# Attention and greedy expert routing on one core: four of the 24 deferred turns of x move from the first routing search to the stretch ahead of it

## Chip, cores and metric

The kernel runs on one core of a Trainium2 chip, in one launch. The metric is device time in microseconds (us) of a whole execution; the median of the runs counts. The engines are called PE (TensorE, matmuls), DVE (VectorE), ACT (ScalarE), POOL (GpSimd) and SP (SyncE, here a queue that issues DMAs).

## What is computed

The reference is attention with a soft cap on the scores, and behind it a layer of eight experts to which tokens are given greedily.

```python
# attention: q, k, v are (8 batches, 12 heads, 448, 64)
scores = cap * tanh(q @ k.T / sqrt(64) / cap)
attn   = exp(scores - max); attn /= sum(attn) + 1e-9
x      = (attn @ v).transpose(0,2,1,3).reshape(3584, 768)

# experts: capacity 448 tokens each
logits = x @ w_gate                       # 3584 x 8
for idx in argsort(-logits.flatten()):    # best pair first
    tok, e = divmod(idx, 8)
    if not assigned[tok] and counts[e] < 448: assign tok to e
for e in range(8):
    out[mask_e] = relu(x[mask_e] @ w1[e]) @ w2[e]
```

## The kernel before

The attention part (`attention`, up to some 331 us of the profiled execution) goes through 24 groups of four heads, three groups to a batch of tokens. For each group PE makes scores (line 190, 195), ACT applies tanh and exp (196, 201), DVE adds the exponentials (207), and PE multiplies them with v (231). The result for a batch is `xT`, x with its 768 features on partitions. From `xT` and the sums PE makes the logits of the batch (252; for the very last group 167), which are turned token-major by four transposes with `ident` (267). DVE divides and adds them (273 to 289) and writes the routing keys of the batch (`propose_a`, 498 to 509; the last key is `r_VA`).

x itself must lie in DRAM (`xs`) token-major, so that an expert's tokens can be gathered. One **turn** does that for one pair of heads of one batch (`xt`, lines 26 to 57): four PE transposes into one PSUM bank (37), then a copy out of the bank. For the batches 0 to 3 this happens inside the attention loop. For the last four batches (`NDEF=4`) it is deferred: 24 turns, each with the four transposes into a `psL` bank, a copy by ACT to a buffer `raw` (49), a multiply by POOL with the reciprocals `rin` into `xn` (52), and after some of them a write `xs<-xn` from the SP queue (56). Only the last turn of all is done by ACT alone (43) with a write from ACT's own queue (44). Batches 4 and 5 had been spilled to DRAM (`xd`) and are read back as `xTr` (30), both at the first deferred turn.

The deferred turns fill the first routing search. A search finds the threshold of the best 448 tokens of an expert in three phases A, B and C of 5, 6 and 5 steps (`select`). Here a step is named by phase and number: A1 to A5, B1 to B6, C1 to C5. A step is a chain: DVE and ACT compare the turned keys with three thresholds and count (`cmpD`, `cmpA`, lines 560 to 566), PE adds the counts over partitions (572, "the count"), DVE picks the next threshold (576, `fl`). Ahead of A1 PE turns the keys `r_VA` (536) and DVE casts them (534). In phase B, and just ahead of it, four matmul pieces of attention that are left over (`avs`, line 236 into `psX`) are issued in single steps, one each behind the counts of A5, B2, B4 and B6. After C5 `finalise` makes the token list `idx` (722), POOL gathers the tokens (871), and the first expert's matmuls (894, 965) begin.

The order is written out by hand: within `tc.manual_schedule` each engine executes in the order of the code. The loop of `ffn_all` sets how many turns are issued behind the count of each step:

```python
N0=1; UN=[1,2,1,2,1,2,1,2,1,2,1,2,1,1,2,0]; AN=(4,6,8,10)
...
step()
units(2)
while len(res)<1:
    step()
    if rt.pos=='B':            # behind a count
        if not deferred: warm(2)
        if m in AN: ...        # a left-over piece of attention
        units(UN[m%len(UN)]); m+=1
    elif rt.pos=='A': posts()  # behind the compares: the copies of the turns issued before
```

So ACT's copies of a step's turns stand behind ACT's compare of the next step. There are two `psL` banks and four `raw` buffers.

Of the kernel before, what the change touches and what calls it, by code (L numbers as in the profile page):

```python
# [14 lines left out]
DL=1; DD=[4]  # L15
FA=2
EB=3
def attention(nc, tc, c1, xp, ep, nv, pM, q, k, v, cap, w_gate, xs, L1, ident, on_logits, on_turn, NDEF, xd, setup, mark):

    B,H,S,D=q.shape
# [1 line left out]
    N=B*NQ  # L24
    xT={}; rin={}; xn={}; spilled={}; todo=list(range(B-NDEF,B-2))
    def xt(b,p,late=None):
        if late and todo:
            for n in todo:
                xT[n]=late[1].tile([128,NP,S],F32,name="xTr",bufs=len(todo))
                nc.sync.dma_start(xT[n],spilled[n])  # L30
            todo.clear()
        if p==0:
            alt=late and (b in spilled and (b-B)%2 or b==B-1)
            xn[b]=(late[1] if alt else xp).tile([CP,NJ,H,D],F32,name="xn",bufs=1)
# [24 lines left out]
    with ExitStack() as ctx:  # L59
# [247 lines left out]
        for g in range(N):  # L307
# [53 lines left out]
            if g: av_out(g-1,0); av_out(g-1,1)  # L361
            if m==2 and late and b<B-1: logit(bb,0,3)
        g=N-1; b=B-1
        rnd(b,R[0],True,False); rnd(b,R[1],False,False); rnd(b,R[2],False,True)
        logit_in(b)
        vround(0); vround(1)
# [2 lines left out]
        lgs[b]=xp.tile([128,S],F32,name="lg",bufs=1); ps=misc.pop(B)  # L369
        nc.vector.tensor_copy(lgs[b],ps[:,:S])  # L370
        ps=pT.tile([128,512],F32,name="psA")
        av(g,0,3,ps,3,2)
        logit(b,2,3,part=part)
        for j in range(3): av(g,0,j,ps,3,2)
    avs=[lambda ps,j=j: av(N-1,1,j,ps,0,3) for j in range(4)]
    return [lambda pool,b=b,p=p: xt(b,p,pool) for b in [B-2]+list(range(B-3,B-NDEF-1,-1))+[B-1] for p in range(NP)],avs


YL=[]
# [6 lines left out]
class Routing:  # L386
# [160 lines left out]
    def select(s,wp,Vt,ab,mid=None,post=None):  # L547
# [6 lines left out]
        for i in range(steps):  # L554
# [16 lines left out]
            ps=s.psum()  # L571
# [10 lines left out]
            if i==steps-1:  # L582
                s.tA=t0
                if ab=="C": s.row(s.tA)
            s.pos='B'; yield s.hB; s.pos=''
    def search(s,wp,turned=()):
        nc=s.nc; v=nc.vector
        post=None
        if s.cur==0:
            ps=s.spare(); s.cps={}; o=128  # L590
            for n in "ABC":
                S=s.steps[n]; s.cps[n]=ps[:,o:o+3*S].rearrange("p (s k) -> p s k",k=3); o+=3*S
                nc.scalar.activation(s.cps[n][:,1:],s.C[n][:,1:],AF.Copy)
        if turned:
            for h in range(s.NC//16):
                if ("VA",h) not in turned: s.turn("VA",h)
# [158 lines left out]


W1B=4; W2B=6
def ffn_all(nc, tc, ctx, rt, xs, xz, wg, w1, w2, out, ident, E, wp, deferred, xctx, gen, avs):
    C=448; DM=768; DC=6; DF=1024; FC=8; HD=384
    TS=[(0,128),(128,128),(256,128),(384,64)]  # L760
    wa=ctx.enter_context(tc.tile_pool(name="wa",bufs=W1B))
# [33 lines left out]
    rt.early=early  # L795
    zero_ix=wp.tile([16,1],I32,name="zix",bufs=1); nc.vector.memset(zero_ix,0)
    first_rows=wp.tile([16,E],F32,name="frow",bufs=1)
    N0=1; UN=[1,2,1,2,1,2,1,2,1,2,1,2,1,1,2,0]; AN=(4,6,8,10)
    ctx.enter_context(tc.manual_schedule(engines={ET.PE,ET.Activation,ET.DVE,ET.Pool,ET.SP}))
    pa=pt.tile([128,512],F32,name="psX")  # L800
    m=0
# [1 line left out]
    def warm(n,t=None):  # L803
        if not t:
            if not wu[0]: wu[0]=pt.tile([128,512],F32,name="psX")
            t=wu[0]
        for _ in range(n): nc.tensor.matmul(t[:,:128],ident,ident,start=True,stop=True)
    rt.warm=warm; rt.spare=lambda: wu[0]; rt.since=lambda: now[0]-end[0]; rt.place=lambda: now[0]%320
    warm(0)
    step()  # L810
    units(2)
    while len(res)<1:
        step()
        if rt.pos=='B':
# [249 lines left out]
def full(nc,tc,q,k,v,cap,wg,w1,w2,out):  # L1064
    with ExitStack() as ctx:
        cp=ctx.enter_context(tc.tile_pool(name="cp",bufs=1))
        dr=ctx.enter_context(tc.tile_pool(name="dr",bufs=1,space=bass.MemoryType.DRAM))
        xs=dr.tile([3584,768],F32,name="xs")
        NDEF=4
        xd=dr.tile([2 if NDEF<4 else NDEF-2,128,6,448],F32,name="xd")  # L1070
        xz=[dr.tile([n,768],I16,name=f"xz{i}") for i,n in enumerate((512,384))]
        ident=cp.tile([128,128],F32,name="ident"); make_identity(nc,ident)
        L1=cp.tile([112,32,8],F32,name="L1")
        r=Routing(nc,cp,3584,8); r.ident=ident; r.tc=tc
        xctx=ExitStack()
        xp=xctx.enter_context(tc.tile_pool(name="xp",bufs=2,side="right"))
        ep=xctx.enter_context(tc.tile_pool(name="ep",bufs=2,side="right"))
        nv=xctx.enter_context(tc.tile_pool(name="nv",bufs=5,side="right"))
        pM=xctx.enter_context(tc.tile_pool(name="pM",bufs=2,space=PSUM,side="right"))
        r.psum=lambda: pM.tile([128,512],F32,name="psM")  # L1080
        turned=set()
        def on_logits(b):
            (r.propose if b<7 else r.propose_a)(L1,4*b,4*b+4)
        def on_turn(b):
            if b==3:
                r.turn("VA",b//4); turned.add(("VA",b//4))
        r.mark=[None]
        deferred,avs=attention(nc,tc,cp,xp,ep,nv,pM,q,k,v,cap,wg,xs,L1,ident,on_logits,on_turn,NDEF,xd,r.setup,r.mark)
        wp=ctx.enter_context(tc.tile_pool(name="wp",bufs=2))
        pp=ctx.enter_context(tc.tile_pool(name="pp",bufs=2,space=PSUM))  # L1090
        r.pp=pp; r.pm=pM; del r.psum
        px=xctx.enter_context(tc.tile_pool(name="px",bufs=2,space=PSUM,side="right"))
        xr=xctx.enter_context(tc.tile_pool(name="xr",bufs=4,side="right"))
        deferred=[lambda f=f: f((px,xr)) for f in deferred]
        ffn_all(nc,tc,ctx,r,xs,xz,wg,w1,w2,out,ident,8,wp,deferred,xctx,r.phases(wp,L1,turned),avs)


_INS=["q","k","v","cap","moe_w_gate","moe_w1","moe_w2"]
# [24 lines left out]
```

## Time and profile before

| | us |
|---|---|
| median of 3 runs | 881.8 (880.81 to 882.2) |
| profiled execution, its own time | 885.21 |
| its span, first to last instruction | 883.4 |
| busy: PE / DVE / ACT / POOL | 858.3 / 587.2 / 585.2 / 374.3 |

The busy times are shares of the whole span: PE looks busy at 97%, but the chain of work that ended last runs through DVE, ACT, POOL and DMAs from some 327 to 387 us, where the attention ends and the experts' matmuls have not begun.

### The profile page before, as it was taken

To read this page: it belongs to the slowest core of one execution; us is meant where nothing else is said; L and a number is where in the kernel's file an instruction comes from. 1 tells how busy PE (TensorE), PEld (TensorE's weight loads), DVE (VectorE), ACT (ScalarE), POOL (GpSimd) and SP (SyncE) were. 2 spreads that over 40 slices of the span, in tenths; PEclk is the share of its full clock that TensorE was granted. 3 is DMA by queue.
4 is the path that set the end of the run, shared out by engine and by line. 5 is a ranking of instruction groups with operands and counts; after the bars stand their busy time and mean duration, and the time that the engine had idled before them with its cause. 6 is when DMAs were issued, how large, how long until landed. Compare 5 with 4: busy or idle time off the path is not lost.

```text
span 883.4 us, 17514 instructions
## 1 busy us (share of the span) xinstructions
PE 858.3 (97%) x6180; PEld 624.6 (71%) x6180; DVE 587.2 (66%) x2027; ACT 585.2 (66%) x832; POOL 374.3 (42%) x535
## 2 busy tenths in 40 slices
PE   6999999999999998989999999999999999999997
PEld 3334444444333435878988989989989989999997
DVE  3878898989897878756786777777767753130210
ACT  6999898989899968355384673664655745435521
POOL 8010000000000009464475496594674767756841
PEclk9999999999999999899999999999999999999999
DMA  9979998596995017770942883955935927929701
GB/s 136 153 121 148 187 138 166 94 181 97 227 181 83 1 57 246 203 221 1 287 125 54 220 263 111 262 164 161 279 111 171 310 81 192 309 66 243 229 10 53
DMA packets 339496, 140.05 MB, mean 159 GB/s; under 512 B 261232, under 2 KB 329456, under 8 KB 338896
## 3 DMA queue, kind: packets, MB, share of 16 engines
q1 hardware_dynamic: 328736, 109.03, 56.3%
q0 software_dynamic: 4688, 22.02, 7.4%
q10 hardware_dynamic: 5984, 7.88, 2.5%
q8 instruction: 48, 0.79, 0.4%
q14 instruction: 40, 0.33, 0.1%
HBM read 97.61 MB, written 33.03 MB: 148 GB/s over the span
## 4 chain that ended last, share of the span: by engine, by line
PE 84%; ACT 4%; issue 4%; DVE 3%; DMA 2%; POOL 1%; POOLq 0%; ACTq 0%; DVEq 0%
PE psH L965 26%; PE psH L996 25%; PE psA L231 12%; PE psS L190 11%; PE psM L252 3%; ACT e L196 2%; PE psS L195 2%; ACT e L201 2%; DMA w1r<-in_moe_w_dram 1%; PE psM L37 1%; DMA q<-in_q_dram 1%; PE psL L37 1%; PE psM L267 1%; POOL xg L871 1%; DVE cmpD L564 0%
## 5 line engine op out<-in xcount | busy, mean ns | idle before, releaser
L996 PE MATMUL psH<-w2h,hh 128*128 128x384 f32 x896 | 234.9, 340 | 0.0
L196 ACT ACTIVATE e<-psS 128x896 f32<-128x896 f32 x168 | 147.5, 910 | 30.0 <-PE psS L190 15.8
L996 PE MATMUL psH<-w2l,hh 128*128 128x384 f32 x512 | 165.8, 339 | 0.0
L996 PEld LDWEIGHTS psH<-w2h,hh 128*128 128x128 f32 x896 | 161.8, 188 | 0.1
L201 ACT ACTIVATE e<-e,bias 128x1792 f32<-128x1792 f32 (+2 forms) x74 | 147.3, 1991 | 1.8
L965 PE MATMUL psH<-xgh,w1h 128*128 128x448 f32 (+1 forms) x384 | 143.3, 373 | 0.1
L965 PE MATMUL psH<-xgh,w1l 128*128 128x448 f32 (+1 forms) x384 | 141.7, 369 | 0.0
L965 PE MATMUL psH<-xgl,w1h 128*128 128x448 f32 (+1 forms) x384 | 137.1, 370 | 0.0
L190 PE MATMUL psS<-tq,tk 64*64 64x448 f32 x1152 | 129.5, 544 | 7.5 <-ACT e L196 5.3
L849 POOL TENSOR_TENSOR w1l<-w1r,w1h 128x768 fp32r<-128x768 f32 x62 | 114.2, 1842 | 44.8 <-ACT w1h L842 42.5
L231 PE MATMUL psA<-e,nv 64*64 64x448 f32 x1104 | 120.8, 539 | 0.0
L849 POOL TENSOR_TENSOR w2l<-w2r,w2h 128x768 fp32r<-128x768 f32 x64 | 117.9, 1842 | 3.0 <-ACT w2h L842 2.9
L514 POOL TENSOR_SCALAR r_Bt<-r_b 112x4 f16<-112x4 int32 x1 | 0.2, 199 | 264.1 <-DVE rin L289 264.1
L207 DVE TENSOR_TENSOR es<-es,e 64x896 f32<-64x896 f32 (+2 forms) x70 | 96.0, 1372 | 2.7 <-ACT e L201 1.5
L996 PEld LDWEIGHTS psH<-w2l,hh 128*128 128x128 f32 x512 | 95.8, 188 | 0.1
L190 PEld LDWEIGHTS psS<-tq,tk 64*64 64x64 f32 x1152 | 42.8, 132 | 73.5 <-issue 36.8
L973 DVE SCALAR_TENSOR_TENSOR hh<-psH,hh 128x64 fp32r<-128x64 f32 (+1 forms) x128 | 44.1, 386 | 74.2 <-ACT hh L971 73.3
L971 ACT ACTIVATE hh<-psH 128x448 fp32r<-128x448 f32 x64 | 34.7, 542 | 84.6 <-PE psH L965 79.5
L231 PEld LDWEIGHTS psA<-e,nv 64*64 64x64 f32 x1104 | 44.5, 133 | 59.2 <-issue 51.6
L965 PEld LDWEIGHTS psH<-xgh,w1h 128*128 128x128 f32 x384 | 72.9, 190 | 8.0 <-issue 2.6
L965 PEld LDWEIGHTS psH<-xgh,w1l 128*128 128x128 f32 x384 | 72.7, 189 | 5.3
L965 PEld LDWEIGHTS psH<-xgl,w1h 128*128 128x128 f32 x384 | 72.7, 190 | 5.2 <-DVE xgl L928 0.2
(389 smaller groups left out, 1270.4 us busy)
## 6 DMA issues: line engine op xcount, KB each, us to landing
w1r<-in_moe_w_dram SPq DMA_DIRECT2D x64, 384.0 KB, 5.2
w2r<-in_moe_w_dram SPq DMA_DIRECT2D x64, 384.0 KB, 6.9
k<-in_k_dram SPq DMA_DIRECT2D x92, 112.0 KB, 3.4
q<-in_q_dram SPq DMA_DIRECT2D x92, 112.0 KB, 3.8
nv<-in_v_dram SPq DMA_DIRECT2D x72, 128.0 KB, 3.7
xz<-pl ACTq DMA_DIRECT2D x18, 384.0 KB, 3.0
xs<-xn SPq DMA_DIRECT2D x4, 1344.0 KB, 7.2
xd<-xT SPq DMA_DIRECT2D x2, 1344.0 KB, 6.1
```

The source lines that it names most:

```text
L37: nc.tensor.transpose(ps[:CP,j*128:(j+1)*128],xT[b][:,p,j*CP:(j+1)*CP],ident)
L190: for c in range(2): nc.tensor.matmul(ps[c*64:c*64+64,h,:S],tks[g,0][hp,o,u*128+c*64:u*128+c*64+64],tks[g,1][hp,o,:],start=True,stop=True)
L196: nc.scalar.activation(ev(g,r),ps[:,:,:S],AF.Tanh,scale=sr[0])
L201: act=lambda: nc.scalar.activation(e,e,AF.Exp,scale=sr[1],bias=bias)
L207: t=es_t[g]; add=lambda o,a,b: nc.vector.tensor_tensor(o,a,b,op=ALU.add)
L231: nc.tensor.matmul(avp[g,o][h*64:h*64+64,:S],lhs,rhs[hp,h,:],start=(j==0 and x==0),stop=j==3)
L252: nc.tensor.matmul(ps[g*32:g*32+32,:S],lhs,rhs,start=first,stop=last)
L849: (eng or nc.gpsimd).tensor_tensor(view(l),r,view(h).bitcast(F32),op=ALU.subtract)
L965: nc.tensor.matmul(ps[:,o:C],a[:,c,:],b[:,c,o:],start=(m==0 and o==0),stop=(m==DC*3-1)); m+=1
L971: nc.scalar.activation(h[:,:C],ps[:,:C],AF.Relu)
L973: nc.vector.scalar_tensor_tensor(h[:,d:d+b-a],ps[:,a:b],0.0,h[:,a:b].bitcast(F32),op0=ALU.max,op1=ALU.subtract)
L996: nc.tensor.matmul(ps[:,:HD],h[:,f,a:a+128],spl[p,2,hf,f//2][w][:,f%2,:],start=(m==0),stop=(m==nm-1))
```

## The change

The turns of batch 6 for the first four head pairs leave the search. The first stands ahead of the last group's first matmul with v (and so ahead of the transposes of the last logits), the second and third behind those transposes, the fourth (`held`) behind the last matmul with v. They use the PSUM banks of the attention scores (`psS`, two turns to a tile of two banks) and free `nv` buffers instead of `psL` and `raw`. The copy of the fourth is issued in `ffn_all`. The three small copies of constants by ACT (`consts`) move to a `psM` bank and behind the last logits. The other 20 turns are spread over the search with one or two to a step, and the last one stands in C5's place where `warm(2)` stood. The spilled batches are read back one by one: batch 5 at the first turn that is left, batch 4 at batch 6's last.

```diff
     def xt(b,p,late=None):
-        if late and todo:
-            for n in todo:
-                xT[n]=late[1].tile([128,NP,S],F32,name="xTr",bufs=len(todo))
-                nc.sync.dma_start(xT[n],spilled[n])
-            todo.clear()
+        if late and todo and len(late)<3 and (len(todo)==NDEF-2 or b==B-2 and p==NP-1):
+            n=todo.pop()
+            xT[n]=late[1].tile([128,NP,S],F32,name="xTr",bufs=NDEF-2)
+            nc.sync.dma_start(xT[n],spilled[n])
...
+        rest=[(bb,p) for bb in [B-2]+list(range(B-3,B-NDEF-1,-1))+[B-1] for p in range(NP)]
+        two=[None,0]
+        class Banks:
+            def tile(s,*a,**kw):
+                if not two[1]: two[0]=pS.tile([128,2,512],F32,name="psS")
+                two[1]^=1
+                return two[0][:,1-two[1],:]
+        class Rows:
+            def tile(s,*a,**kw): return nv.tile([128,3,2*HG,D],F32,name="nv").rearrange("p j h d -> p (j h d)")[:CP,:512]
+        def one(): return xt(*rest.pop(0),(Banks(),Rows(),False))
...
         ps=pT.tile([128,512],F32,name="psA")
+        u=one(); u()
         av(g,0,3,ps,3,2)
         logit(b,2,3,part=part)
+        consts(pM)
+        for _ in range(2): u=one(); u()
         for j in range(3): av(g,0,j,ps,3,2)
+        held=one()
...
+    def consts(s,pool):
+        ps=pool.tile([128,512],F32,name="psM"); s.cps={}; o=0
+        for n in "ABC":
+            S=s.steps[n]; s.cps[n]=ps[:,o:o+3*S].rearrange("p (s k) -> p s k",k=3); o+=3*S
+            s.nc.scalar.activation(s.cps[n][:,1:],s.C[n][:,1:],AF.Copy)
...
-        if s.cur==0:
-            ps=s.spare(); s.cps={}; o=128
-            for n in "ABC":
-                S=s.steps[n]; s.cps[n]=ps[:,o:o+3*S].rearrange("p (s k) -> p s k",k=3); o+=3*S
-                nc.scalar.activation(s.cps[n][:,1:],s.C[n][:,1:],AF.Copy)
...
-    N0=1; UN=[1,2,1,2,1,2,1,2,1,2,1,2,1,1,2,0]; AN=(4,6,8,10)
+    N0=1; UN=[1,1,1,2,1,1,1,1,1,2,1,2,1,1,1,1]; AN=(4,6,8,10)
...
-    warm(0)
     step()
-    units(2)
+    units(1)
+    held()
```

How this moves instructions is shown at three places. The first is PE from the last logits' matmuls (`vgs`) to the turn of the keys `r_VA`, before:

```order
L167 MATMUL psM<-e_3368,vgs 32x448 x8
L236 MATMUL psA<-e_3368,nvh 64x448 x2
L267 MATMUL psM<-ident,lg 112x128 x4
L236 MATMUL psA<-e_3320,nv 64x448 x2
L236 MATMUL psA<-e_3346,nv 64x448 x2
L236 MATMUL psA<-e_3368,nv 64x448 x2
L536 LDWEIGHTS r_VA
L536 MATMUL psR<-r_id_352,r_VA 128x112
```

The same stretch of PE in the changed kernel (its lines 235, 266 and 549 are the old 236, 267 and 536; line 36 is the old 37):

```order
L36 MATMUL psS<-ident,xT 112x128 x4
L235 MATMUL psA<-e_3368,nvh 64x448 x2
L266 MATMUL psM<-ident,lg 112x128 x4
L36 MATMUL psS<-ident,xT 112x128 x8
L235 MATMUL psA<-e_3320,nv 64x448 x2
L235 MATMUL psA<-e_3346,nv 64x448 x2
L235 MATMUL psA<-e_3368,nv 64x448 x2
L36 MATMUL psS<-ident,xT 112x128 x4
L549 LDWEIGHTS r_VA
L549 MATMUL psR<-r_id_352,r_VA 128x112
```

One turn (four transposes) now stands ahead of the last logits' transposes, and three more between them and the turn of the keys. With the counters that an instruction waits for, the turn of the keys reads in the changed kernel:

```order
L36 MATMUL psS<-ident,xT 112x128 [waits Activation_49]
L36 MATMUL psS<-ident,xT 112x128 x3
L549 LDWEIGHTS r_VA [waits DVE_49]
L549 MATMUL psR<-r_id_352,r_VA 128x112 [waits Activation_49]
L36 MATMUL psL<-ident,xT 112x128 x4
```

The `psR` bank that it writes is one that the fourth turn's `psS` tile held, and the count of ACT that it waits for is that of the fourth turn's copy; the corresponding matmul of before waits for nothing but DVE's `r_VA`. The second place is ACT in the same stretch, from the last exponential to the first compare, before:

```order
L201 ACTIVATE e_3368<-e_3368,bias 128x896
L593 ACTIVATE psX<-r_CA 128x12
L593 ACTIVATE psX<-r_CB 128x15
L593 ACTIVATE psX<-r_CC 128x12
L237 ACTIVATE xT<-psA 128x448
L560 ACTIVATE cmpA,r_cd_323<-r_VAt,r_T0A 128x252
L49 ACTIVATE raw<-psL 112x512 x2
```

and in the changed kernel (48 is the old 49, 236 the old 237, 573 the old 560):

```order
L200 ACTIVATE e_3368<-e_3368,bias 128x896
L48 ACTIVATE nv<-psS 112x512
L603 ACTIVATE psM<-r_CA 128x12
L603 ACTIVATE psM<-r_CB 128x15
L603 ACTIVATE psM<-r_CC 128x12
L48 ACTIVATE nv<-psS 112x512 x2
L236 ACTIVATE xT<-psA 128x448
L48 ACTIVATE nv<-psS 112x512
L573 ACTIVATE cmpA,r_cd_323<-r_VAt,r_T0A 128x252
L48 ACTIVATE raw<-psL 112x512
```

The four copies to `nv` are new here, and the fourth stands behind the copy of the last attention result and ahead of the first compare. The third place is the SP queue at the read-back, as a piece of the difference:

```order
-L30 DMA xTr<-xd 128x2688 x2
-L56 DMA xs<-xn 112x4x512
-L56 DMA xs<-xn 112x4x256
+L30 DMA xTr<-xd 128x2688
+L55 DMA xs<-xn 112x4x512
+L30 DMA xTr<-xd 128x2688
+L55 DMA xs<-xn 112x4x256
```

The second read-back now stands behind the first write of x, which waits for POOL's multiply of the fourth turn.

## Rows read from the trace of the kernel before

**Rows 1.** The chain of work that ended last, in order of time, from the last logits to the first expert: start us, us, what.

```profile
330.54 0.19 DVE r_VA L507
...
362.59 0.19 DVE idx L722
...
363.90 0.98 POOL xg L871
...
373.28 3.48 DMA w1r<-in_moe_w_dram
...
387.41 3.15 PE psH L965 x9
```

**Rows 2.** The timeline of PE from 326.5 to 331.3 us: start us, us, engine, line, operation, out<-in, count, and in brackets the idle time before and what ended it.

```profile
326.67 0.97 PE L236 MATMUL psA<-e,nvh 64*64 64x448 f32 x4
327.57 0.65 PE L267 MATMUL psM<-ident,lg 128*112 128x128 f32 x4
328.14 2.48 PE L236 MATMUL psA<-e,nv 128*64 128x448 f32 x12
330.79 0.22 PE L536 MATMUL psR<-r_id,r_VA 112*128 112x112 f16 x1 [0.17 <-DVE r_VA L507]
```

**Rows 3.** The timeline of all engines, same columns: DVE's copy of the last logits, the issue of the two read-backs on SP's queue, ACT's copy of the last attention result, two turns in one go ahead of A1's count, and one turn later on with ACT's copy behind it.

```profile
326.80 0.62 DVE L370 COPY lg<-psM 128x448 f32<-128x448 f32 x1
...
326.84 0.82 SPq L30 DMA_DIRECT2D xTr<-xd  x2
...
330.67 0.54 ACT L237 ACTIVATE xT<-psA 128x448 f32<-128x448 f32 x1 [7.27 <-PE psA L236]
...
331.26 1.09 PE L37 MATMUL psL<-ident,xT 128*112 128x128 f32 x8 [0.25 <-ACT xT L237]
...
338.64 0.65 PE L37 MATMUL psL<-ident,xTr 128*112 128x128 f32 x4
...
339.38 0.60 ACT L49 ACTIVATE raw<-psL 112x512 f32<-112x512 f32 x1 [0.19 <-PE psL L37]
```

**Rows 4.** The same timeline: the threshold picks of A1, A2, A3, then of B2 to B4 and B6, then of C4 and C5. Their distance is the length of a step.

```profile
332.52 0.16 DVE L576 SCALAR_TENSOR_TENSOR fl<-psR,r_HA 128x4 f32<-128x4 f32 x1 [0.27 <-PE psR L572]
...
333.92 0.16 DVE L576 SCALAR_TENSOR_TENSOR fl<-psR,r_HA 128x4 f32<-128x4 f32 x1
...
335.23 0.16 DVE L576 SCALAR_TENSOR_TENSOR fl<-psR,r_HA 128x4 f32<-128x4 f32 x1
...
341.02 0.16 DVE L576 SCALAR_TENSOR_TENSOR fl<-psR,r_HB 128x4 f32<-128x4 f32 x1
...
342.54 0.16 DVE L576 SCALAR_TENSOR_TENSOR fl<-psR,r_HB 128x4 f32<-128x4 f32 x1 [0.35 <-PE psR L572]
...
343.94 0.16 DVE L576 SCALAR_TENSOR_TENSOR fl<-psR,r_HB 128x4 f32<-128x4 f32 x1 [0.23 <-PE psR L572]
...
346.82 0.16 DVE L576 SCALAR_TENSOR_TENSOR fl<-psR,r_HB 128x4 f32<-128x4 f32 x1 [0.23 <-PE psR L572]
...
353.35 0.16 DVE L576 SCALAR_TENSOR_TENSOR fl<-psR,r_HC 128x4 f32<-128x4 f32 x1
...
354.76 0.16 DVE L576 SCALAR_TENSOR_TENSOR fl<-psR,r_HC 128x4 f32<-128x4 f32 x1 [0.24 <-PE psR L572]
```

**Rows 5.** The timeline of PE from the count of B2 to that of B3: count, left-over piece of attention, one turn, count.

```profile
340.81 0.18 PE L572 MATMUL psR<-r_cd,r_bo 128*128 128x4 bf16 x1
340.92 0.97 PE L236 MATMUL psX<-e,nv 128*64 128x448 f32 x4
341.82 0.65 PE L37 MATMUL psL<-ident,xTr 128*112 128x128 f32 x4
342.30 0.17 PE L572 MATMUL psR<-r_cd,r_bo 128*128 128x4 bf16 x1
```

**Rows 6.** Groups of instructions by line from 331.2 to 356.3 us, the search: line, engine, operation, names, shapes, count | busy us, mean ns | idle us before, and what ended it.

```profile
L52 POOL TENSOR_TENSOR xn<-raw,rin 112x512 f32<-112x512 f32 x23 | 23.3, 1049 | 0.1
L49 ACT ACTIVATE raw<-psL 112x512 f32<-112x512 f32 x23 | 12.8, 587 | 1.1 <-PE psR L572 0.9 <-PE psL L37 0.2
```

**Rows 7.** DMA issues by line in single narrow windows (KB each, median us from issue to landing): the first read-back, the second, the first write of x from SP's queue, and the last one from ACT's.

```profile
xTr<-xd SPq DMA_DIRECT2D x1, 1344.0 KB, 5.6
...
xTr<-xd SPq DMA_DIRECT2D x1, 1344.0 KB, 8.5
...
xs<-xn SPq DMA_DIRECT2D x1, 896.0 KB, 5.2
...
xs<-xn ACTq DMA_DIRECT2D x1, 448.0 KB, 3.7
```

**Rows 8.** Busy time of each engine in three stretches, phase A, the later phase C, and `finalise`: stretch, its length, busy us of PE, PEld, DVE, ACT and POOL, PE's granted clock as a share of full speed, the DMA engines' share, GB/s.

```profile
331.20:338.00 6.80, 5.47 (x43) 4.01 (x45) 5.70 (x39) 6.42 (x19) 6.47 (x12) 1.00 0.59 247
347.00:353.70 6.70, 4.75 (x37) 3.11 (x34) 5.43 (x35) 5.84 (x18) 6.70 (x7) 1.00 0.78 239
353.70:360.50 6.80, 6.18 (x31) 5.80 (x30) 4.68 (x25) 3.58 (x12) 3.39 (x4) 0.50 0.80 237
```

**Rows 9.** The timeline at the end of the search: ACT's eight small copies of the last turn, and in `finalise` DVE's last operand for the index matmuls and PE's load for the first of them, which stands behind 16 warming matmuls.

```profile
354.73 1.74 ACT L43 ACTIVATE xn<-psL,rin 112x64 f32<-112x64 f32 x8
...
359.39 0.42 DVE L706 TENSOR_TENSOR oi<-oh,r_idc 112x512 f16<-112x512 f16 x1
...
360.58 0.40 PEld L710 LDWEIGHTS <-oi 112*128 112x128 f16 x4
```

More of the change, by code (lines that the diff above doesn't have):

```diff
@@ L17, with attention @@
 EB=3
-def attention(nc, tc, c1, xp, ep, nv, pM, q, k, v, cap, w_gate, xs, L1, ident, on_logits, on_turn, NDEF, xd, setup, mark):
+def attention(nc, tc, c1, xp, ep, nv, pM, q, k, v, cap, w_gate, xs, L1, ident, on_logits, on_turn, NDEF, xd, setup, mark, consts):
     B,H,S,D=q.shape
@@ L371, in attention @@
         ps=pT.tile([128,512],F32,name="psA")
+        u=one(); u()
         av(g,0,3,ps,3,2)
         logit(b,2,3,part=part)
+        consts(pM)
+        for _ in range(2): u=one(); u()
         for j in range(3): av(g,0,j,ps,3,2)
+        held=one()
     avs=[lambda ps,j=j: av(N-1,1,j,ps,0,3) for j in range(4)]
-    return [lambda pool,b=b,p=p: xt(b,p,pool) for b in [B-2]+list(range(B-3,B-NDEF-1,-1))+[B-1] for p in range(NP)],avs
+    return [lambda pool,b=b,p=p: xt(b,p,pool) for b,p in rest],avs,held
 YL=[]
@@ L757, with ffn_all @@
 W1B=4; W2B=6
-def ffn_all(nc, tc, ctx, rt, xs, xz, wg, w1, w2, out, ident, E, wp, deferred, xctx, gen, avs):
+def ffn_all(nc, tc, ctx, rt, xs, xz, wg, w1, w2, out, ident, E, wp, deferred, xctx, gen, avs, held):
     C=448; DM=768; DC=6; DF=1024; FC=8; HD=384
@@ L807, in warm @@
         for _ in range(n): nc.tensor.matmul(t[:,:128],ident,ident,start=True,stop=True)
-    rt.warm=warm; rt.spare=lambda: wu[0]; rt.since=lambda: now[0]-end[0]; rt.place=lambda: now[0]%320
-    warm(0)
+    rt.warm=warm; rt.since=lambda: now[0]-end[0]; rt.place=lambda: now[0]%320
     step()
-    units(2)
+    units(1)
+    held()
     while len(res)<1:
@@ L1087, in full @@
         r.mark=[None]
-        deferred,avs=attention(nc,tc,cp,xp,ep,nv,pM,q,k,v,cap,wg,xs,L1,ident,on_logits,on_turn,NDEF,xd,r.setup,r.mark)
+        deferred,avs,held=attention(nc,tc,cp,xp,ep,nv,pM,q,k,v,cap,wg,xs,L1,ident,on_logits,on_turn,NDEF,xd,r.setup,r.mark,r.consts)
         wp=ctx.enter_context(tc.tile_pool(name="wp",bufs=2))
@@ L1094, in full @@
         deferred=[lambda f=f: f((px,xr)) for f in deferred]
-        ffn_all(nc,tc,ctx,r,xs,xz,wg,w1,w2,out,ident,8,wp,deferred,xctx,r.phases(wp,L1,turned),avs)
+        ffn_all(nc,tc,ctx,r,xs,xz,wg,w1,w2,out,ident,8,wp,deferred,xctx,r.phases(wp,L1,turned),avs,held)
 _INS=["q","k","v","cap","moe_w_gate","moe_w1","moe_w2"]
```

## Prediction, made without having seen the changed kernel run

> **What bounds the kernel now.** I read the chain of waits first, to see which part of the program the moved turns can touch. Between the attention and the first expert it does not run through PE's amount of work: it goes from the last logits' transposes over DVE to the keys `r_VA` (330.54), through the sixteen steps of the search to `idx` (362.59), then through the gather (363.90) and the expert's weights (373.28) to the first expert's matmuls (387.41) [rows 1]. The gather needs `idx`, so whatever moves `idx` moves all that follows by the same amount, and I price the change at `idx`.
>
> Next I read PE's timeline just ahead of the search, because three of the four turns go there, into what looks like a wait for the last logits. The reader is to see that this place is nearly full: the logits' transposes start at 327.57, the twelve matmuls with v at 328.14 and take 2.48, and the turn of the keys follows at 330.79, with a wait of only 0.17 for `r_VA` [rows 2]. The 2.65 us in which DVE makes the keys hold 2.48 us of matmuls. It is ACT that is idle there, 7.27 us before 330.67 [rows 3].
>
> Then the search. Two neighbouring picks of a threshold are 1.31 us apart where nothing disturbs (A2 to A3). The other distances are 1.40 (A1 to A2), 1.52 and 1.40 (B2 to B3 to B4), 2.88 for two steps (B4 to B6) and 1.41 (C4 to C5) [rows 4]. So most turns are hidden behind DVE's part of a step; what a thinner search can give back is bounded by these excesses over 1.31: 0.09 + 0.21 + 0.09 + 0.26 + 0.10 = 0.75, an estimate, as not every step has its row here.
>
> **The change, part by part.** *Turn 1* stands ahead of the last logits' transposes. These wait for DVE's copy `lg`, which ends at 326.80 + 0.62 = 327.42 [rows 3], and start at 327.57, when PE comes free: 0.15 us of room. A group of four transposes costs 328.14 - 327.57 = 0.57 from start to start [rows 2]. Nothing waits long enough to hide it, so the logits' transposes start at 328.14, and DVE's chain to `r_VA` ends at 330.73 + 0.57 = 331.30. That is the first term, and it is on the path by any reading but for the 0.15.
>
> *Turns 2 and 3* follow the transposes. Eight transposes in one go took 1.09 where four took 0.65 [rows 3], so 0.44 for each further turn, 0.88. The matmuls with v start at 328.14 + 0.57 + 0.88 = 329.59 and end at 332.07. *Turn 4* (`held`) follows at about 332.00 (a next group starts some 0.07 ahead of the modelled end: 326.67 + 0.97 against 327.57 [rows 2]) and ends 0.65 later, at 332.65.
>
> *The turn of the keys* now waits for ACT's copy of turn 4, as the order shows, since it writes a bank of that `psS` tile. ACT first copies the last attention result, 0.54 [rows 3], from about 332.12 to 332.66, then turn 4. A copy started 339.38 - (338.64 + 0.65) = 0.09 after its transposes and took 0.60 [rows 3]; I put it from 332.74 to 333.33. With 0.06 from that to PE, as from the end of `r_VA` (330.73) to 330.79 [rows 1, 2], the turn of the keys is at 333.39 instead of 330.79: **+2.60**. DVE's keys lie ready from 331.30, 2.1 us before. The stall has moved from DVE's chain to PE and ACT. Queued behind this matmul on PE are the first search turn and A1's count; behind the copy on ACT is A1's compare; DVE has nothing else to do.
>
> *The search.* Four turns fewer. A step that already has 1.31 gains nothing. A1 to A2 and C4 to C5 lose a double turn; I give each at most 0.1. A step with a left-over piece of attention is bound by PE: count, piece 340.92 to 341.82, turn 341.82 to 342.30, count [rows 5]; it keeps its piece and its turn, so it keeps its 1.52, and the step behind it too. B5 and C1 keep double turns. Sum: **-0.2**, against the other bound of -0.75.
>
> *POOL* multiplies four turns before it makes the keys of phases B and C. Its 23 multiplies of 1049 ns fill the search (23.3 us, idle 0.1), yet ACT's copies are held up by PE and not by POOL [rows 6]; with four done early it only gets ahead. I cost it at nothing. Those keys of B and C are read a whole phase later. *The constants'* copies lie in ACT's idle stretch; nothing.
>
> *The read-backs.* The first is issued as before, at 326.84 [rows 3], and lands 5.6 later [rows 7], ahead of its first use in A2. The second now stands on SP's queue behind the first write of x, which waits for POOL's multiply of turn 4, 333.4 to 334.4. The write lands 5.2 after its issue, and the second read-back of before, issued some 0.4 behind the first, landed 8.5 + 0.4 - 5.6 = 3.3 after it [rows 7]. That gives 334.4 + 5.2 + 3.3 = 342.9. It is first needed by the turn behind B2's count, before at 341.82 [rows 5], now at 341.82 + 2.6 - 0.1 = 344.3. Room of 1.4, so nothing; if it needed a full 8.5 behind the write, it would land at 348.1 and hold up PE, and with it the search, by 3.8. I take the first value, since the 8.5 of before holds the first read-back too, and none runs beside the second now.
>
> *The last write of x* starts behind ACT's eight copies, 1.74 us [rows 9], which now follow C5's turn and not C4's, one step (1.4) later. It lands 3.7 after its issue [rows 7], by my count 0.9 ahead of `idx`. Nothing, but this is the thinnest cover.
>
> **Sum.** +2.60 - 0.2 = +2.4. Against the profiled execution of 885.2 that is 887.6. It is 3.4 above the median of 881.8; I apply the same difference to the median: **884.2**.
>
> **A rule weighed.** In phase A PE runs hardly anything but transposes and counts, is busy for 5.47 of 6.80 us, and the granted clock is 1.00, its level of 2.4 GHz; behind the later phase C, busy for 4.75 of 6.70, it is 0.50, which is 1.2 GHz [rows 8]. Phase A has nine turns before and seven after, so PE's busy time there falls to about 5.47 - 2 x 0.44 = 4.6, close to that second row. That is the third rival below. The Trainium skill ("TensorE: Matmul & The Clock Gate", section "Part 4: PE-mode transpose") says that transposes do not count as PE activity in the way matmuls do; by that, taking some away would not change the clock, and the sum would stay 884.2. The row of phase A disagrees, as far as it goes: it holds its full clock on transposes. The same page's section "HAM oscillation — how this bites in real kernels" has the clock fall where PE is left waiting; by that the third rival would come true, and the 0.7 us that PE now waits ahead of the keys count for it.
>
> **The rivals.**
>
> *First, it is no slower: the turns fit in the waits.* If the three turns ran in PE's gaps and the fourth's copy were done before the keys are ready (331.30), only the 0.57 of turn 1 would stand against 0.2 to 0.75 from the search: +0.4 to -0.2, 881.6 to 882.2. It decides at the point where PE's added work between the logits' transposes and the keys, 0.88 + 0.57, with the copy behind it fits beside DVE's chain. Against it: 2.48 of the 2.65 us are taken [rows 2], and the order has a wait on ACT's copy. For it: modelled ends of PE, which may hide more room than the rows show, and ACT's 7.27 us of idle. Chance 0.21.
>
> *Second, the second read-back comes late* by part of the 0 to 3.8 us. At about half, 1.9: 886.1. For it: the wait behind a write that itself waits for POOL; against it the room of 1.4. Chance 0.07.
>
> *Third, the clock.* If it falls in phase A, a step with a left-over piece, 0.90 + 0.48 of PE work [rows 5], gets 1.38 longer. The low level lasted 6.8 us in [rows 8], enough for two such steps: +2.8, 887.0. For it the 4.6 of 6.8 above; against it that phase A is followed by the pieces themselves. Chance 0.06.
>
> *Fourth, faster.* `finalise` runs at half clock, and PE's load of `oi` starts at 360.58, 0.77 behind the end of `oi` at 359.81 [rows 9], held by warming matmuls. A turn in C5's place could keep the clock full and give back that 0.77 and more of the index matmuls behind it; with the first rival's sum that would be 880 or less. Alone, on the forecast's sum, it gives 883.4. Chance of the fast case 0.04.
>
> **How the numbers follow.** The forecast has 0.62. Its own range is 883.2 (the excess of 0.75 given back and another 0.4 of room on PE) to 885.4 (no saving, and some 1 us of the bounds above). 0.2%, 1.76 us, is about what a measurement of this kernel can tell from no change: below 880.0 is faster, above 883.6 slower. Of the forecast's 0.62 some 0.08 lie below 883.6. Faster: 0.05 with a remainder. Same: 0.21 + 0.08 = 0.29. Slower: 0.54 + 0.07 + 0.06 = 0.67, of which I take 0.66. The range reaches down into the first rival, to 881.4, and up to the second, 886.2; outside are the third, the fourth and half of the second's tail.
>
> **What would show it.** In the changed trace the last logits' transposes start some 0.57 later against the keys' chain, the turn of the keys at about 333.4 with ACT's `nv` copy as what ended its wait, the steps keep 1.31, 1.40 and 1.5, `idx` stands at about 365.0 and the first expert at 389.8. The second read-back lands before the turn behind B2 needs it, and the last write before `idx`. The prediction is wrong if the wait of the keys' turn is ended by DVE's `r_VA`, if the steps shrink below 1.31, or if the distance from `idx` to the first expert changes.

## The result, and the profile after

The changed kernel takes 886.5 us in the median (885.9 to 888.15, 6 runs), the kernel before on the same chip 881.35 (6 runs). The ratio is 1.0055, 95% interval 1.0045 to 1.0065: slower by 4.85 us by the ratio and by 5.15 by the two medians, where 2.4 was forecast. (881.35 x 1.0055 is 886.2, the figure that several texts below use for the changed kernel.) The sign and the mechanism at the keys are as forecast; the size is twice that. The 886.2 is the upper end of the prediction's range, and the median lies 0.3 above it.

The timeline of the changed kernel from the first moved turn to the search, PE and ACT's copy of the fourth turn (columns as in [rows 2]):

```profile
326.69 0.65 PE L36 MATMUL psS<-ident,xT 128*112 128x128 f32 x4
...
328.17 0.65 PE L266 MATMUL psM<-ident,lg 128*112 128x128 f32 x4
...
329.62 2.48 PE L235 MATMUL psA<-e,nv 128*64 128x448 f32 x12
...
332.02 0.65 PE L36 MATMUL psS<-ident,xT 128*112 128x128 f32 x4
...
332.71 0.60 ACT L48 ACTIVATE nv<-psS 112x512 f32<-112x512 f32 x1
...
333.36 0.21 PE L549 MATMUL psR<-r_id,r_VA 112*128 112x112 f16 x1 [0.69 <-ACT nv L48]
```

These answer to [rows 2]: the last logits' transposes at 328.17 (forecast 328.14), the matmuls with v at 329.62 (329.59), the fourth turn at 332.02 (332.00), its copy by ACT from 332.71 (332.74), the turn of the keys at 333.36 (333.39), its wait ended by that copy. The profile's chain of waits puts the start of the copy down to the landing of the first read-back (326.86 + 5.85 = 332.71). But the copy ahead of it on ACT ends only at 332.14 + 0.54 = 332.68, so the read-back can have held it by 0.03 us at most, and in a_both and a_mul_both below the chain has the transposes in that place.

DVE and POOL in the same stretch show what was not forecast:

```profile
329.96 2.09 POOL L51 TENSOR_TENSOR xn<-nv,rin 112x512 f32<-112x512 f32 x2 [0.80 <-ACT nv L48]
330.16 0.90 DVE L512 TENSOR_TENSOR r_P<-L,r_m 112x32 f16<-112x32 f32 x1
...
331.10 1.00 DVE L514 TENSOR_TENSOR r_P<-r_P,r_e8m 112x32 f16<-112x32 f16 x1
...
332.66 0.19 DVE L520 TENSOR_TENSOR r_VA<-r_P,r_At 112x32 f16<-112x32 f16 x1
```

Two operations of DVE take 0.90 and 1.00 us. POOL's two multiplies end at some 331.0 and at 332.05, and each of the two ends right behind one of them. `r_VA` starts at 332.66 and ends at 332.85, not at 331.30.

The picks of A1, A2, A4, A5, C4 and C5 and `idx`, as in [rows 4]:

```profile
335.01 0.16 DVE L589 SCALAR_TENSOR_TENSOR fl<-psR,r_HA 128x4 f32<-128x4 f32 x1 [0.27 <-PE psR L585]
...
336.31 0.16 DVE L589 SCALAR_TENSOR_TENSOR fl<-psR,r_HA 128x4 f32<-128x4 f32 x1
...
338.94 0.16 DVE L589 SCALAR_TENSOR_TENSOR fl<-psR,r_HA 128x4 f32<-128x4 f32 x1
...
341.02 0.16 DVE L589 SCALAR_TENSOR_TENSOR fl<-psR,r_HA 128x4 f32<-128x4 f32 x1 [0.91 <-PE psR L585]
...
356.53 0.16 DVE L589 SCALAR_TENSOR_TENSOR fl<-psR,r_HC 128x4 f32<-128x4 f32 x1
...
357.83 0.16 DVE L589 SCALAR_TENSOR_TENSOR fl<-psR,r_HC 128x4 f32<-128x4 f32 x1
...
366.20 0.19 DVE L735 TENSOR_REDUCE idx<-r_ixf 128x4 int32<-128x32 f32 x1
```

A1 to A2 fell from 1.40 to 1.30, as forecast. But A4 to A5 is 2.08 us, and C5 to `idx` is 8.37, against 362.59 - 354.76 = 7.83 in the first profile of before [rows 1, 4]. Busy time and clock ahead of and in the two places (columns as in [rows 8]):

```profile
330.50:337.30 6.80, 4.21 (x29) 2.15 (x25) 5.73 (x32) 4.02 (x11) 5.13 (x12) 1.00 0.48 160
351.00:357.80 6.80, 4.20 (x35) 2.90 (x33) 5.55 (x39) 6.01 (x18) 6.50 (x7) 1.00 0.82 252
357.80:364.60 6.80, 6.03 (x30) 5.57 (x31) 3.86 (x19) 2.67 (x10) 2.18 (x2) 0.50 0.55 163
```

PE is busy for 4.21 and 4.20 of 6.80 us in the first two stretches, and behind each the clock falls to 0.50 (1.2 GHz): from 337.35 to 340.76 and from 357.83 to 364.65. In the first fall the two turns of A4 show it, in the timeline and then in the chain of waits (start, us, what):

```profile
339.09 1.86 PE L36 MATMUL psL<-ident,xTr 128*112 128x128 f32 x8
```

```profile
339.30 1.65 PE psL L36 x8
```

In the timeline eight transposes took 1.09 us at full clock [rows 3] and take 1.86 here; DVE waits 0.91 us for the count behind them. In the second fall the chain runs through the 16 warming matmuls of `finalise`, which stand ahead of the index matmuls:

```profile
360.53 3.62 PE psX L820 x16
```

In the second profile of the kernel before, which comes next, it runs through DVE's `oi` in that place.

### The profile page after: what moved, and what is told of

The parts are those of the page before. It is cut to its first block, busy times and chain, and to the rows that moved or that the text cites. A ratio compares the mean times of both kernels' runs of the same rounds, so it can differ in the third digit from the quotient of the medians.

```text
span 884.1 us, 17509 instructions
## 1 busy us (share of the span) xinstructions
PE 857.3 (97%) x6176; PEld 624.2 (71%) x6176; DVE 589.0 (67%) x2027; ACT 586.6 (66%) x832; POOL 375.2 (42%) x535
## 4 chain that ended last, share of the span: by engine, by line
PE 80%; ACT 5%; DMA 5%; issue 4%; DVE 4%; POOL 1%; SPq 0%; ACTq 0%; POOLq 0%; DVEq 0%
PE psH L978 26%; PE psH L1009 22%; PE psA L230 11%; PE psS L189 10%; PE psM L251 3%; ACT e L195 2%; ACT e L200 2%; PE psS L194 2%; PE psM L36 1%; DMA xg<-xs,idx 1%; DMA q<-in_q_dram 1%; DVE es L206 1%; DMA xg<-xz 1%; DMA w1r<-in_moe_w_dram 1%; DVE cmpD L577 1%
## 5 line engine op out<-in xcount | busy, mean ns | idle before, releaser
L51 POOL TENSOR_TENSOR xn<-nv,rin 112x512 f32<-112x512 f32 x4 | 4.2, 1058 | 263.8 <-ACT psM L603 261.7
```

## The experiments

**b2: the kernel before, a second profile.** No edit.

> The kernel before, once more, for a second profile of it: its first one took 885.2 us where its median is 881.4. Expected: ratio 1.000, and a profile in which the stretch from the threshold search to idx is as in the first (idx at 362.6), while the time that is missing (some 3 us) shows behind idx, in the weight reads and the gather ahead of the first expert. If the search itself is shorter in the second profile, the comparison of the two first profiles is off by that much.

Median 881.76, ratio 1.0004 (0.9991 to 1.0017). The profiled execution took 882.5 us. Its clock stays full from 21 to 881 us, and the stretches of the first profile read (phase A, the later phase C, `finalise`):

```profile
331.60:338.40 6.80, 5.44 (x43) 4.00 (x45) 5.70 (x39) 6.42 (x19) 6.44 (x13) 1.00 0.59 246
348.30:355.10 6.80, 4.64 (x39) 3.34 (x37) 5.52 (x40) 6.01 (x19) 6.80 (x8) 1.00 0.77 239
355.10:361.90 6.80, 4.88 (x41) 4.26 (x41) 4.82 (x23) 2.51 (x10) 2.43 (x3) 1.00 0.88 251
```

The last picks and `idx` in it:

```profile
353.79 0.16 DVE L576 SCALAR_TENSOR_TENSOR fl<-psR,r_HC 128x4 f32<-128x4 f32 x1
...
355.09 0.16 DVE L576 SCALAR_TENSOR_TENSOR fl<-psR,r_HC 128x4 f32<-128x4 f32 x1
...
361.89 0.19 DVE L722 TENSOR_REDUCE idx<-r_ixf 128x4 int32<-128x32 f32 x1
```

Not all was as expected: C5 to `idx` is 6.80 us, not 7.83, and C4 to C5 1.30, not 1.41. Of the 2.7 us by which this profile's span is shorter (880.7 against 883.4), 0.7 lies up to `idx` and 2.0 behind it, where all of it was expected. So the first profile was of an execution in which the clock had fallen ahead of `finalise`, and of this kernel that is the exception: the mean clock over the 17 runs of it beside this one is 0.997 in the median, over the six of the changed kernel 0.992 (0.989 to 1.000 and 0.990 to 0.994).

Take this profile as the kernel before. From the turn of the keys (331.23 in this one, all of which runs 0.44 later than the first) the parts up to `idx` are:

| | forecast | changed against b2 |
|---|---|---|
| turn of the keys | +2.60 | 333.36 - (331.23 - 0.44) = +2.57 |
| keys to A4's pick | -0.1 | 5.58 - 5.75 = -0.17 |
| A4 to A5 | 0 | 2.08 - 1.30 = +0.78 |
| A5 to C5 | -0.1 | 16.81 - 16.81 = 0 |
| C5 to `idx` | 0 | 8.37 - 6.80 = +1.57 |
| sum | +2.4 | +4.75 |

Up to `idx`, then, half of the loss is the forecast's wait for the keys, and the other half is the two stretches in which the clock was low. That the sum is near the measured 4.85 is in part chance: the two profiled executions differ by only 3.4 us (885.9 and 882.5), because part of the 4.75 is given back behind `idx`. The chains of waits from the gather to the first expert, of b2 and then of the changed kernel:

```profile
365.98 6.13 DMA xg<-xs,idx
...
386.25 1.93 PE psH L965 x9
```

```profile
369.42 4.41 DMA xg<-xs,idx
...
389.30 1.93 PE psH L978 x9
```

From `idx` to the last of these rows, which is the row with which [rows 1] ends, it takes 24.82 us in the first profile, 24.36 in b2 and 23.10 in the changed kernel. Of the 4.75 some 3.5 arrive there (389.30 against 386.25 - 0.44).

For the whole time, what the clock costs is read from executions of one kernel. Among those of the kernel before that were taken beside the runs below, the seven with a mean clock of 0.993 took 882.8 us in the median, the 41 with 0.997 or 0.998 took 881.4. Of the changed kernel, the two with 0.990 took 887.2 and 888.2, the two with 0.994 took 885.9 and 886.2. By that the 0.005 between the two kernels' median clocks go with 1.6 to 2.0 us, an estimate; a part of the 4.85 stays unassigned.

**Three kernels with the second read-back where the change put it.** The first, a_three, sends the fourth turn back into the search:

```diff
-        held=one()
+        held=lambda: None
-    UN=[1,1,1,2,1,1,1,1,1,2,1,2,1,1,1,1]
+    UN=[1,1,2,2,1,1,1,1,1,2,1,2,1,1,1,1]
```

The second, a_mul, leaves the turns and moves POOL's multiplies of the early ones behind POOL's part of the keys; a_three_mul has both edits:

```diff
+            if late and len(late)==3: return lambda: mult(src,h0)
...
-        u=one(); u()
+        ms=[]; u=one(); ms.append(u())
...
-    held()
+    late.insert(0,held())
```

> The changed kernel with three turns ahead of the search and the fourth back in it (A3 gets two). The turn of the keys then no longer waits for the copy of a fourth turn. Theory 1 (the copy holds the keys by 0.45 us only, since DVE's keys are themselves late, 332.66, because two of DVE's operations took 0.90 and 1.00 us beside POOL's multiplies of the three turns): the turn of the keys at 332.9 instead of 333.4, and the time 0.4 to 0.5 us below the changed kernel's 886.2. Rival (DVE's two long operations are not tied to what POOL does there, or are not in the way): PE sets it, behind the matmuls with v, at 332.05, and the time falls by 1.3.

> The changed kernel with POOL's multiplies of the four early turns moved behind POOL's part of the keys; the turns and ACT's copies stay. Theory 1: DVE's two operations fall back from 0.90 and 1.00 to 0.19 each, r_VA is there at 331.2 instead of 332.66, but the turn of the keys still waits for ACT's copy of the fourth turn and stays at 333.36: the time changes by less than 0.2 us. Rival (what holds the keys is DVE and not the copy): the turn of the keys comes at 332.05 and the time falls by 1.3.

> Both of the last two edits: three turns ahead, and POOL's multiplies behind its part of the keys. Theory 1: neither ACT's copy nor DVE is in the way, and the turn of the keys comes where PE comes free of the matmuls with v, at 332.05: 1.3 us below the changed kernel, some 884.9, still 1.3 at the keys behind the kernel before. Rival (the two lateness terms add up and nothing else is there): 331.3 or earlier, 2.1 below the changed kernel.

All three came out slower than the changed kernel: 888.7 (ratio to before 1.0072), 889.3 (1.0091) and 891.1 (1.0108). At the keys they did what theory 1 says. In a_three, whose whole front runs 0.40 later than the changed kernel's, DVE's late keys are what ends the wait, at the 332.9 that was expected plus this 0.40 (the other two are repeated below without a second disturbance):

```profile
333.30 0.22 PE L549 MATMUL psR<-r_id,r_VA 112*128 112x112 f16 x1 [0.81 <-DVE r_VA L520]
```

But each made the first write of x later, and with it the second read-back behind it on SP's queue, issued at 336.53, 337.68 and 338.20 instead of 334.84. The turn behind B2's piece of attention then waits for it; this is a_three_mul, PE's timeline:

```profile
342.56 0.97 PE L238 MATMUL psX<-e,nv 128*64 128x448 f32 x4
347.99 1.07 PE L36 MATMUL psL<-ident,xTr 128*112 128x128 f32 x4 [4.46 <-DMA xTr<-xd]
```

In a_three the same wait is 1.99 us, in a_mul 1.76. The time from the read-back's issue to its landing in a_three:

```profile
xTr<-xd SPq DMA_DIRECT2D x1, 1344.0 KB, 9.6
```

In a_mul it is 10.0. In the changed kernel there is no such wait: the turn starts at 345.00, right behind the piece. Its landing is missing from this trace. In a_warm and a_warm2 below, which issue it where the changed kernel does, it took 9.8 and 10.0. At 9.6 to 10.0 it lands at 344.4 to 344.8 in the changed kernel, an estimate from those rows. The cover is 0.2 to 0.6 us, not the 1.4 of the prediction.

**The same with both read-backs at the front.** a_both is the changed kernel with this edit alone; a_mul_both and a_three_mul_both are two of the kernels above with it:

```diff
-        if late and todo and len(late)<3 and (len(todo)==NDEF-2 or b==B-2 and p==NP-1):
+        while late and todo and len(late)<3:
             n=todo.pop()
```

> The changed kernel with both read-backs issued at the front, ahead of the first write of x. In the changed kernel's trace the second read-back causes no wait (the turn behind B2 starts right behind the piece of attention, at 345.00), so theory 1 (it is free there): the time stays within 0.5 us of the changed kernel's 886.2. Rival (it is late in some executions; in three other kernels it landed 9.6 to 10.0 us after its issue, and by that would land at 344.4, only 0.6 ahead of its use): 0.5 to 1 us faster.

> The kernel a_mul (POOL's multiplies of the four early turns behind POOL's part of the keys) with both read-backs at the front. Its wait of 1.8 us for the second read-back behind B2 must go. Theory 1 (ACT's copy of the fourth turn holds the keys, whatever DVE does): the turn of the keys as in the changed kernel, 333.4, and the time as a_both's within 0.5 us. Rival: below a_both by 1 us or more.

> The kernel a_three_mul (three turns ahead, multiplies late) with both read-backs at the front. Its wait of 4.5 us behind B2 must go. Theory 1: the turn of the keys where PE comes free of the matmuls with v, 1.3 us ahead of the changed kernel's, and the time 1.3 below a_both's, if the clock behaves as there. If the clock stays full more often, up to 2 us below.

a_both: 886.3, ratio 1.0053 (1.0039 to 1.0066). The read-backs one by one cost nothing in the changed kernel, thin as the cover is.

a_mul_both: 885.97, ratio 1.0056 (1.0041 to 1.0071). Its DVE and its turn of the keys:

```profile
330.16 0.19 DVE L518 TENSOR_TENSOR r_P<-L,r_m 112x32 f16<-112x32 f32 x1
...
331.12 0.19 DVE L526 TENSOR_TENSOR r_VA<-r_P,r_At 112x32 f16<-112x32 f16 x1
...
333.35 0.21 PE L555 MATMUL psR<-r_id,r_VA 112*128 112x112 f16 x1 [0.69 <-ACT nv L48]
```

With POOL's multiplies out of the way DVE's operation takes 0.19 again and `r_VA` ends at 331.31, the forecast's 331.30. The turn of the keys does not move, and neither does the time: it is ACT's copy of the fourth turn that holds it.

a_three_mul_both: 883.94, ratio 1.0026 (1.0014 to 1.0039), 2.4 us below a_both. Without the fourth turn and with DVE free the keys come where PE is done with v:

```profile
332.11 0.22 PE L553 MATMUL psR<-r_id,r_VA 112*128 112x112 f16 x1
```

That is 1.35 ahead of a_both's 333.46, as expected (1.3). The other 1.0 is more than theory 1 had; 0.77 of it lies in the search up to `idx` (365.33 against 367.45 in a_both, 2.12 earlier), where the profiled a_both had its clock down for 6.8 us in phase A and a left-over piece of attention in that stretch, which took 1.76 us instead of the 0.97 of [rows 5]:

```profile
341.05 1.76 PE L235 MATMUL psX<-e,nv 128*64 128x448 f32 x4
```

That is the third rival's case as it was priced, in one execution. That the 1.0 comes from there is not shown: the two profiled executions differ by 0.6 us only (885.78 and 885.15).

**The clock.** a_warm adds idle matmuls ahead of the turn of eight steps, a_warm2 behind it, a_best puts the latter into a_three_mul_both (without the step A3, which has two turns there). The lines are those of a_warm2; a_warm has three and not four at B1 and B3:

```diff
-    AN=(4,6,8,10)
+    AN=(4,6,8,10); WM={0:4,1:4,2:4,5:4,7:4,12:4,13:4,14:4}
...
-            units(UN[m%len(UN)]); m+=1
+            units(UN[m%len(UN)])
+            warm(WM.get(m,0)); m+=1
```

> The changed kernel with three or four matmuls of ident with ident, whose results nothing reads, behind the counts of A1, A2, A3, B1, B3, C2, C3 and C4, where PE would wait. Theory 1 (a part of the loss is PE's clock, which in the changed kernel's trace stood at 1.2 GHz from 337.3 to 340.8 and from 357.8 to 364.7, and in the second profile of the kernel before nowhere in the search): the clock stays at 2.4 GHz, A4 to A5 falls from 2.08 us to 1.3, C5 to idx from 8.4 to 6.8, and the time falls by 2.3 us to some 883.9. Rival (the clock is a by-product and costs nothing): the time stays at 886.2, or grows by what the added matmuls delay the counts, 0.1 each.

> The kernel a_warm once more, with the four idle matmuls of a step behind its turn and not ahead of it: in a_warm they stood ahead of the turn, ACT's copy and its next compare came later by them, and the steps that held them took 1.43 to 1.47 us where they had taken 1.30. Theory 1 (the clock is the rest of the loss): full clock in the search as in a_warm, steps of 1.31 as in the changed kernel, C5 to idx in 6.8 us, and the time 2.3 us below 886.2, some 883.9. Rival (more PE work costs as much as the clock gives back, wherever it stands): 886 as a_warm.

> Every cause undone that the runs so far show, with three turns still ahead of the search: no fourth turn there, POOL's multiplies behind its part of the keys, both read-backs at the front (all as in a_three_mul_both, 883.9), and the idle matmuls of a_warm2. Theory 1: what is left is PE's work ahead of the keys, +1.3 us against the kernel before, less 0.2 in the search: some 882.5, a ratio of 1.001. Rival (something else in the change costs too): 883.9 as without the idle matmuls.

a_warm: 886.09, ratio 1.0046 (1.0032 to 1.0059). Mean clock 0.998, and full throughout the search and `finalise` in its profile; C5 to `idx` is 6.87 us and A4 to A5 1.34, as theory 1 has them. From the keys to `idx` it takes 31.41 us where the changed kernel takes 32.84. That is 1.43 and not 2.35, because the steps with idle matmuls take 1.43 to 1.47 where they had taken 1.30. Yet the median moved by 0.4 at most, and by the ratios by 0.8.

a_warm2: 885.55, ratio 1.0043 (1.0028 to 1.0058). The steps still take 1.38 to 1.42. The trace shows why:

```profile
335.24 1.06 PE L820 MATMUL psX<-ident 128*128 128x128 f32 x8
```

Four idle matmuls are eight instructions of PE and 1.06 us, so with the turn they fill the step. The turn behind B2 also waited 0.30 us for the second read-back. The clock fell only at 360.3, inside `finalise`, for 3.4 us.

a_best: 884.72, ratio 1.0036 (1.0020 to 1.0052); 882.5 was expected. It is no faster than a_three_mul_both without the idle matmuls (883.94), as the rival had it. The four of its twelve executions with a mean clock of 0.999 or more took 882.4 to 884.3, the others 884.4 to 887.6.

Where a_warm's gain at `idx` goes is seen in its chain of waits:

```profile
379.19 8.43 DMA w1r<-in_moe_w_dram
...
389.20 2.71 PE psH L979 x9
```

`idx` comes 0.95 us earlier than in the changed kernel, and the first expert's weights `w1r` are asked for 1.0 earlier (the changed kernel's row is 380.20, 7.53). But the read takes 8.43 us, so the matmuls behind it start only 0.1 earlier. Then the clock falls, and they take 2.71 us instead of 1.93. Such a last fall, for 3.4 us in the first expert, begins between 387.8 and 391.1 in the first profile of before, in a_warm, a_warm2 and a_best, and `idx` to the end of the span takes 520.6 to 521.2 us there; in the other ten profiles there is none, and the stretch takes 516.6 to 518.9. Why a kernel that kept its clock in the search should lose it there, no run tells apart. So a_warm shows what the clock costs up to `idx`, and not that holding it there is worth as much in the whole time: its five executions, with mean clocks of 0.998 to 1.000, took 885.05 to 887.66.

b_warm2 tried the idle matmuls in the kernel before.

```diff
+    AN=(4,6,8,10); WM={0:3,2:3,12:3,13:3}
...
+            warm(WM.get(m,0)); m+=1
```

> The kernel before with three idle matmuls behind the turn of A1, A3, C2 and C3. In most of its executions its mean clock is 0.997 or more, and in the one that was profiled first the clock fell ahead of finalise and C5 to idx took 7.8 us where the second profile has 6.8. Theory 1: it holds its clock already, so the median stays at 881.5 and at most the slower executions come nearer to it: ratio 0.999 to 1.000. Rival (the clock is lost in most executions): 1 us faster, 0.9988 or less.

887.21, ratio 1.0056 (1.0039 to 1.0073), and it says nothing on the clock: in the kernel before the constants of the search lie in the PSUM bank that the idle matmuls write, and DVE's compare reads them from there.

```profile
334.45 0.45 DVE L564 SCALAR_TENSOR_TENSOR cmpD<-r_VAt,th,psX 128x224 bf16<-128x224 f16 x1 [1.42 <-PE psX L807]
```

A1 to A2 takes 2.69 us by it. It also shows what moving `consts` to a bank of its own is good for.

**a_spread: the turns set otherwise in the search.** a_three_mul_both, with nine turns in phase A and six in each of B and C:

```diff
-    UN=[1,1,2,2,1,1,1,1,1,2,1,2,1,1,1,1]
+    UN=[1,2,1,2,1,1,1,1,1,1,1,2,1,1,1,1]
-    units(1)
+    units(2)
```

> The kernel a_three_mul_both with its 21 turns set otherwise in the search and no idle matmuls: phase A gets nine, as in the kernel before, phase C six, as there, and what the three early turns save comes out of phase B alone, where the pieces of attention keep PE at work (six turns instead of nine). Theory 1 (the clock falls in phase A of the changed kernel because PE has two turns fewer there): the clock stays at 2.4 GHz in phase A, A4 to A5 takes 1.31 instead of 2.1, and the time falls by 0.8 us below a_three_mul_both's 883.9, to 883.1; if it stays full ahead of finalise too, by 2.3, to 881.7 or so. Rival (the turns in phase A are not what the clock hangs on): the clock falls at 337 us as before and the time stays at 883.9.

884.65, ratio 1.0029 (1.0018 to 1.0041), against a_three_mul_both's 1.0026: no gain. In the profile the clock stays full through phase A and A4 to A5 takes 1.31, as theory 1 says; it falls at 356.6, for 6.8 us, and C5 to `idx` takes 8.26. But A3 to A4 takes 1.97, and the gain is given back there:

```profile
337.38 0.60 ACT L48 ACTIVATE raw<-psL 112x512 f32<-112x512 f32 x1 [0.60 <-POOL xn L54]
337.87 0.50 ACT L577 ACTIVATE cmpA<-r_VAt,th 128x252 bf16<-128x252 f16 x1
```

ACT's copy waits for a `raw` buffer, since POOL has the three postponed multiplies of the early turns ahead of the one that frees it, and A4's compare is queued behind the copy. What PE must do in phase A to keep its clock stays open too. From the turn of the keys on, PE was busy for 2.55 of 4.41 us in a_three_mul_both, where the clock then fell at 336.5, and for 3.23 of 4.50 in a_spread, where it did not. But a_three and a_three_mul, with the same eight turns in phase A as a_three_mul_both and 2.43 and 2.64 of 4.50 us, kept it as well, up to 346.9 and 345.1. With one profile of each, theory 1 of a_spread is not shown.

None of these kernels is faster than the kernel before.

## Why the prediction was right, and what it had too small

**The keys.** Turn 1, turns 2 and 3, turn 4, ACT's two copies and the wait for the second of them: each time in the trace is within 0.03 us of the sum, and the term measured +2.57 for +2.60. a_mul_both shows that the wait is the copy's, a_three_mul_both that without it PE's own work ahead of the keys is left, 1.35 of the 2.57 less. The first rival, that the turns fit in the waits, is refuted by the same rows.

**DVE's chain.** "Ends at 331.30" was wrong by 1.55, and the prediction's "DVE has nothing else to do" overlooked POOL: it priced POOL's multiplies in the search, where they hurt nothing, and not ahead of the keys, where the early copies by ACT start them while DVE makes the keys. The error cost nothing since the copy was later still; in a_three, where the fourth turn's copy is gone, DVE's chain is what holds the keys.

**The search.** A1 to A2 gave 0.10, as forecast; the steps with a piece of attention kept 1.52 (B2 to B3, 344.20 to 345.72). C4 to C5 gave nothing, since b2 has 1.30 there already. But for the clock, a search with four turns fewer is shorter by the 0.17 of the table.

**The clock.** This is the step that failed. The prediction's sum left the clock as it was. It named the place (phase A with two turns fewer), the sign and the rows as the third rival, at 887.0, which is the forecast's sum and 2.8, and gave that 0.06; the measured time is nearer to it than to 884.2. That the time lies at the upper end of the range is luck: the range was drawn up to 886.2 for the second rival, which cost nothing, and the third stood outside. What came is +0.78 in A4 to A5 and +1.57 behind C5. That both are the clock's is shown up to `idx` by a_warm, where with the clock held the two stretches take 1.34 and 6.87; their share of the whole time is not shown. The first of them is smaller than the 2.8 priced, because the low level lasted 3.4 us and mostly met a double turn and not the pieces of attention. The second was missed for a reason in the reading: the profile of before was of an execution 3.4 us above the median, and the prediction carried that difference over to the changed kernel unexamined. Part of it was the clock: `finalise` at half clock [rows 8] is how that one execution went, and 6.80 us instead of 7.83 is how the second profile went. Taken as the rule, it hid that there was a loss still to be had there, and made the fourth rival (faster by a full clock in `finalise`) look possible where the kernel before mostly has it already. Of the two rules that were weighed, neither is borne out as it stands. The one on idle PE (the Trainium skill, "TensorE: Matmul & The Clock Gate", section "HAM oscillation — how this bites in real kernels") tells of a PE that waits longer for a DMA than its matmuls take. Here PE's waits from the turn of the keys to the first fall are 0.59 to 0.79 us each, so the trace goes its way in direction only: PE is less busy, and the clock falls behind it. The one on transposes (the Trainium skill, same page, section "Part 4: PE-mode transpose") has the full clock not engage for them. That does not fit: b2 and a_spread hold the full clock through a phase A made of transposes and counts.

**The read-backs and the last write.** Both were free, as forecast, the first by less than was thought: the landing was put at 5.2 + 3.3 behind the write's issue, and 9.6 to 10.0 from its own issue is what five other runs show. The last write is issued at 361.39, and its landing is missing; with the 3.6 that it takes in a_warm it lands at 365.0, an estimate, 1.2 ahead of `idx`. Where the write came 1.7 to 3.4 us later, the second rival's stall came in full, 1.8 to 4.5 us.

**Behind `idx`.** The prediction priced the change at `idx`, since "whatever moves `idx` moves all that follows by the same amount", and named a changed distance from `idx` to the first expert as a sign of being wrong. That distance did change, from 24.82 us (24.36 in b2) to 23.10. `idx` came at 366.20 instead of 365.0, the first expert at 389.30 instead of 389.8. And in a_both `idx` is 1.25 later than in the changed kernel, with the same span (884.0 and 884.1). The gather and the weights' read stand between, and their times differ from one profile to another.

## What to carry to other kernels

A wait on one engine is room only if the engine that is given the work is idle there itself: here ACT waited 7.27 us while PE had 0.15. Before a profile is taken as the rule, compare its time with the median of the runs: an execution that is 3.4 us off is telling of something (here in part the clock) that the change may turn from exception to rule. When work is moved earlier, follow each of its parts to the end of its queue: the copy, the multiply, the write and the read-back behind the write all moved here, and the copy, the multiply and the read-back were each the next wait in one of the runs. And follow the gain behind the point where it was priced: what is won or lost at `idx` did not all arrive at the first expert.

## What was not expected of the hardware

A DVE operation with two inputs in SBUF waits for a POOL operation that is under way: 0.90 and 1.00 us instead of 0.19, with ends at those of POOL's multiplies. The changed kernel, a_three, a_both, a_warm and a_warm2 show the same; 0.19 is back in every run in which the multiplies were moved. A reduction and an operation with one tensor input beside the same multiplies (at 329.94 and 330.99) kept their 0.19 and 0.16. The Trainium skill ("SBUF — State Buffer", section "Who interferes with whom") says that a DVE instruction with two SBUF inputs contends with a GpSimd instruction that reads SBUF, and that the shared port pair is an exclusive lock; the trace agrees.

A fall of the granted clock lasted 3.4 or 6.8 us in these traces, once 10.2, but for one that is cut off at the end of each. The kernel whose PE work was spread thinner had a mean clock of 0.990 to 0.994 in its six executions, where the kernel before had 0.997 in the median of 17 and single ones down to 0.989: the clock differs from one execution of a kernel to the next, and one profile can mislead.
